# Masks of half of the first layer's score groups added by TensorE, normalised tokens also made by GpSimd, and a new order

## The chip, the cores and the metric

The kernel runs on one core of one Trainium2 chip. The metric is device time in microseconds (us) of one execution; lower is better. A core has five engines with an instruction queue each: TensorE (PE, matrix products into PSUM), VectorE (DVE), ScalarE (ACT), GpSimd (POOL) and SyncE (SP), which here issues all transfers (DMAs). Each engine works through its own queue in order and waits on semaphores where it needs another one's result. In the profile, PEld are PE's weight loads.

## The reference

Two layers, each a sliding-window attention and a token-mixing MLP, on one sequence of 2048 tokens of width 512:

```python
def _A_ref(x, wqkv, wo):
    B, S, D = x.shape
    H = 32; Dh = D // H; W = 256
    qkv = (x @ wqkv).reshape(B, S, 3, H, Dh).transpose(2, 0, 3, 1, 4)
    q, k, v = qkv[0], qkv[1], qkv[2]
    scores = jnp.einsum("bhqd,bhkd->bhqk", q, k) * (Dh ** -0.5)
    idx = jnp.arange(S)
    mask = (idx[:, None] - idx[None, :] >= 0) & (idx[:, None] - idx[None, :] < W)
    p = _softmax(jnp.where(mask[None, None], scores, -1e9), axis=-1)
    o = jnp.einsum("bhqk,bhkd->bhqd", p, v)
    return o.transpose(0, 2, 1, 3).reshape(B, S, D) @ wo

def _B_ref(x, w1, b1, w2, b2):
    h = _layernorm(x, axis=-1)
    u = _gelu(jnp.einsum("bsd,sf->bdf", h, w1) + b1)
    y = jnp.einsum("bdf,fs->bds", u, w2) + b2
    return y.transpose(0, 2, 1)

x = A_x
x = x + _A_ref(_layernorm(x, axis=-1), A_wqkv, A_wo)
x = x + _B_ref(_layernorm(x, axis=-1), B_w1, B_b1, B_w2, B_b2)
x = x + _A_ref(_layernorm(x, axis=-1), A_wqkv, A_wo)
x = x + _B_ref(_layernorm(x, axis=-1), B_w1, B_b1, B_w2, B_b2)
```

Data are bfloat16. The MLP mixes tokens: its first product runs over the 2048 tokens (w1 is 2048 x 1792), its second one gives 2048 tokens back.

## The kernel before

The kernel is written as a graph. Every piece of work is an `op` with an engine, a function that issues its instructions, what it reads and what it writes. The lists `alts` name other engines that could do the same work. A constant, `ORDER`, holds one order of all ops, and for each op which of its alternatives is taken; `replay` reads it, gives out buffers from pools (8 PSUM banks, 7 buffers `pt` of probabilities, and so on) in that order, and `emit` writes each engine's instructions in that order with the semaphore waits that the dependencies and reused buffers ask for. So the order of the work on every engine is written out by hand, as it were, in `ORDER`; nothing is reordered at run time. The `cost` values serve whoever makes the order and have no effect on the chip.

**Attention of a layer.** The queries are cut into chunks: in layer 0 two of 4 blocks of 64 queries and three of 8 (`CHUNKS`, numbered 0 to 4), in layer 1 four of 8. Heads are worked on in four sets `o` of 8 heads. For a chunk, `attention_plan` lists groups of key block by query block tiles: each group fills two pairs of PSUM banks. One score group is one op `f_sc` (matmuls at L679): for each piece four matmuls that run side by side in four row tiles of 32 rows (two heads of 16 each, the keys spread block-diagonally in `kbd`), into four banks. Then come two exponentials on ACT (L694), each over two banks, which write `pt`; then the masks (`f_mask`, L715) on GpSimd, which multiply the diagonal and the far-edge blocks by 0 or 1; then the product with the values (`f_pv`, L732) on PE. A layer has 76 score groups. The pair of each plan's entry `(c0, n, w0)` says where a mask lies and which of its forms it takes. After the products: a transpose on DVE (L752), reciprocal, scaling (`prod`, L758, on GpSimd or DVE), a second transpose, and the output projection (`wo_block`), whose result is added to `x_sb` (L774).

**Around it.** `ln_blocks` computes token statistics (L464, L466, DVE), the inverse deviation (`rstd`, L477, GpSimd) and the normalised tokens `xh_sb` (`normalise`, L484, DVE). `qkv` transposes them (by transfer, or by PE at the start of a layer), projects to q, k and v with matmuls at L506, copies the results out of PSUM (`evq`, `evk`, `evv`, on DVE or ACT) and spreads the keys: for the first 512 tokens of a layer straight from PSUM (`evka`, L574 on ACT, L575 on DVE), later from a staging buffer `stg` into `kbd` (`kz`): by eight small transfers (L595), or by two multiplications with the constants `par` (L600) on GpSimd or DVE. In layer 0 the transfers are allowed for the last quarter of the tokens only.

**Filling PE.** Between score groups PE gets other matmuls, all through the helper at L506: projections, output projections, the first MLP product over the tokens that are ready (`u_part`, evicted at L838 or L842), and in layer 1 the second product of the MLP of layer 0 (`y_block`). After a layer's attention come the rest of the first product (`u_last`, L853, with an addition at L864 and the gelu at L868) and the second product, whose weights are loaded into `pt` and `w2b`; `w2b` holds the partial sums of the first product before that.

Of the kernel before, what the change touches and what calls it, by code (L numbers as in the profile page):

```python
# [7 lines left out]
dt = mybir.dt  # L8
# [3 lines left out]
P = 128  # L12
# [3 lines left out]
    'c-qZYJ&5Dl6~40X%xYimfEE<c1_ks$3o7(L4;)aTLJJCLK>;l&phATU2NZCjfD0ukpa&{ks1U)03KvsM;lhOjQ@C*9VgfE)xNzaZg$ox`xNyLQ3l}-^-'  # L16
    ';DQ%9mqm*W-MJ@-Jf&5^PTUig=m&x8#EXp8bY!nO0MoWh9R2vM_t$7>+eNTltlTbIJQ3qL12EE&*!#1FRrHR{$V`+Fha<*Oj8l@rpfWY<@rHtgZr|~gK'
    '>GZ*|u*d({`H+-*Ru$I5mFHahx4wJ(M<^t+x1172kzX9J-<IS(;`TvM8#W`cBnkFhyRoV8VDjhMOcwGf6@i{tULAvv-6L*7t>4BNl`W%dRJnj#HaVxcO'
    'qaSa6l)qabixrBc~$CzHu^!aeM8wOVCpLhES0nCW_#*=7vWZfDv2$Jsnhr|ERcfK@6w%wQOa836zT_zipG$yi!RnIcu~kI94m_aQR`pSV89{oIJ^e&GA'
    '9y6=af|HhRACumQ@C=84oTo2hWtT&rXYlr9FZ03VS^*BkAKShxjhGDfDR9Ti`s<mp>gS}kabzF|KRvO3Y`V7r>`qrzC$2!Lhw>uapn~Y}Yx>!KPFu$}~'  # L20
    'ih@)%QS0^k!Z!gXr2ucGz_|I`^Nf4L=yna$ghYuVw|!Ho@RdAgnT+Q}G0RvsV{^iCc}_Dev}<i!0PLpL?am3gdov!>H1i0y-E9lkG0yYcvMl#;y<YEj?'
    'i-q3JO9#kSl*0Q>rHfjAN9KT_q|@XJABh0K6E;rp5r+A?H$hD{1yzTrE^>>*Evmt6_YTDqO6r=lC;ZO{AMGh6(Cy>hCw4-HX7hf&=`#*iHP-Tt(Gae7b'
    '{v|GO8d5^73(6Q5Fk%AG1uzVAxkxRqA#n3AW-mo<OLn>$<f#iQ@zsp6e>LS}hC}1t65GqTp3Ml_jbw+cx5)$E^;WtEif$DfF1_GfYoW6uQ$9@7jhba$1'
    '_Ex(y58G+L<9P#`114?H0}u#JaFg2?f_B1tkkkffW8-5ZTDAxR>N49kdUyWNrv#C5}RP=c^J+<^id*OwP^zYk9woA*+TX}aBR!$1c1Oec%QqNrAS{F=V'
    'MzrXDbI0*6XmIlf~uUzksN5Zs6=)^Qa8j=e<)+?-1p;ek5jXG5*bQ&?~U?5-`vl+%I%9F%mQ5Yf&WUAvjt7?veWL48;SrA3X^=L&FAiV+-bPe&UAh{Sa'
    '<@<5J-_K)#t=u&|K@?OpKmj2_jRZl(^ZnE_UBW6vCa3`kVIWt6WS9mZC@+^Z;yCjIXn_DKk>?#r$}*16vg|GNX(Jrp@q8e^<>;*C;*{rQ`KKfaQKME13'
    'O=}m7@%32r2(mR=vWsF?RL8Wf5EU@AY8iv<^@63Qz}sQD1z`Uj4co*Q^l&tfmaAog2!_RAxvb9u_7x=(81Y!Ay22v<phRIr_(*=v?K$eP`j<^T9(POVH'
    'iB&I3|Lc5C7Ij>-E3euzQyM!}tG8M3_*mDHX*LWN{fqI{jC}SglqIK~U|PstT<BzDI+mth(K-^BP)t9=FEyfa)aR2ObOtAPDvV=t>5Cqcc$|but>YwFi'
    'd51S5uLwBCK;RxfHs5fo4qwOUO!1-Do>=?#*E9S)l*G>xoF)tb#Z10`02@};ri`o7h0dCx0Zjli^v(glPhPBbyERcnk5Wb^>s-&ufaWoZg{7R=`s6b;m'
    '^U-wmARQmnxbgHWVRDrz;EU+~;n@qRtUkr#=({&IdMK`QCj&*(GC%%u6rfs)z{IK4vHy{tH`m^#ESe8vSI4|C_%21K|EfDx_(z9(FMlehSDeZJ+pob(5'  # L30
    '2Dea(495WP3W%^y>-u&FoLQ|ph2465({)=spTYFFnM%I_wF9drwK#_StX0;FBFC|JmSHt43&FYd-as~R#dR#mqVHG^a$On~XIjOyfLA^btcNpEqiJjnh'
    'r<oW0f$XPmZ3n@G>$Q78OESuD3TR8Yiv@TP60lQ#u^$q#*W+&b=6Z5Jtt6oV6Pu0!-R}LA^U?qg~9>qclsURDh(($@9rA6KqI=<3TWCp$knxD+kiTRoI'
    '94KJFcKZ)OtnJK%{`8Bn*EPLImUu0}}9p0M3G}xP`3|64$XhSJnAyJ_F{d>SQvT&wwY!aA?eCvwJ8`rgN*1cAgUiP^T&QpCV+WgwZq=v|g?L(IMFL;bg'
    'LG3(#HJhN2iIl4VW?gcleKzrGcC1~JS{H%UR*NCUnMs3Z(0+l>#nAXG(gK{UcG0~LzK@N~Z~Os5EAlq{2oF$&x@%l15!c6;}}?}0MpQ55^w4}u12AlIo'
    'v+8oma4x0!Bnide|p`llJ1@WoId0t)Q6gb~xUaIf{ASx+hu7Q^|fyavNSQ5?C^v1@RiFm>;@k*8(8?@nl9syS4>9n>0V(Tk7N<h+q?_-QdkHhU^Ydk#c'
# [270 lines left out]
def bass_interleave_layers__sliding_block__mixer_token_mlp__prompt_kernel(  # L306
# [12 lines left out]
    F = B_w1.shape[1]  # L319
    assert S == 2048 and D == 512 and F % 256 == 0  # L320
    NT = S // P
    NC = 4
    NFT = F // P
    EPS = 1e-5
    SMSCALE = 0.25
    NPT = 7
    NRL = 4
    NVS = 4
    SPLIT = [True, False]

    CHUNKS = [[(0, 4), (4, 4), (8, 8), (16, 8), (24, 8)], [(0, 8), (8, 8), (16, 8), (24, 8)]]
# [642 lines left out]
```

## Time and profile before

| what | us |
| --- | --- |
| median of 3 runs | 441.83 (441.41 to 443.33) |
| the profiled execution | 441.94 |
| its span on the core | 440.2 |
| first score group starts | 8.77 |
| last score group of layer 0 / layer 1 starts | 151.34 / 352.7 |
| ACT, exponentials: 304, mean of one | 281.5 busy, 1.042 |
| PE, stretch 150 to 200, between the layers | 50.00 busy of 50 |

The span is the time between the first and the last instruction on the core. Layer 0's attention takes roughly the first 155 us, the rest of its MLP about 45, layer 1's attention, with the second product of layer 0's MLP among it, up to 355, and its own MLP the rest. Groups of instructions are named by line, engine, operation and output<-input tile.

The page's slices (each 11 us; a digit is the busy share in tenths) show the stages:

```profile
PE   7998998999999999999999999999999999999996
...
DVE  6999888887887678475768868899987746512223
ACT  5999999999999913618999999999999950420000
POOL 2687898778677610011574877877666631000000
```

### The profile page before, as it was taken

To read this page: it belongs to the slowest core of one execution; us is meant where nothing else is said; L and a number is where in the kernel's file an instruction comes from. 1 tells how busy PE (TensorE), PEld (TensorE's weight loads), DVE (VectorE), ACT (ScalarE), POOL (GpSimd) and SP (SyncE) were. 2 spreads that over 40 slices of the span, in tenths; PEclk is the share of its full clock that TensorE was granted. 3 is DMA by queue.
4 is the path that set the end of the run, shared out by engine and by line. 5 is a ranking of instruction groups with operands and counts; after the bars stand their busy time and mean duration, and the time that the engine had idled before them with its cause. 6 is when DMAs were issued, how large, how long until landed. Compare 5 with 4: busy or idle time off the path is not lost.

```text
span 440.2 us, 13923 instructions
## 1 busy us (share of the span) xinstructions
PE 422.9 (96%) x5992; PEld 187.6 (43%) x5992; DVE 311.1 (71%) x570; ACT 318.5 (72%) x364; POOL 225.4 (51%) x344
## 2 busy tenths in 40 slices
PE   7998998999999999999999999999999999999996
PEld 6543333344333444444444444443443444434452
DVE  6999888887887678475768868899987746512223
ACT  5999999999999913618999999999999950420000
POOL 2687898778677610011574877877666631000000
PEclk9999999999999999999999999999999999999999
DMA  7752423203225365533351651140223346773513
GB/s 243 206 96 64 112 51 66 60 13 72 44 43 147 106 177 158 145 99 78 92 112 37 140 118 25 47 102 17 51 60 86 90 132 179 205 200 112 157 53 101
DMA packets 99885, 45.09 MB, mean 102 GB/s; under 512 B 30064, under 2 KB 99824, under 8 KB 99824
## 3 DMA queue, kind: packets, MB, share of 16 engines
q1 hardware_dynamic: 99824, 44.21, 39.2%
q8 instruction: 47, 0.77, 0.7%
q14 instruction: 14, 0.11, 0.1%
HBM read 33.56 MB, written 2.10 MB: 81 GB/s over the span
## 4 chain that ended last, share of the span: by engine, by line
PE 71%; ACT 19%; DVE 3%; POOL 3%; DMA 2%; issue 1%; SPq 0%; DVEq 0%
PE PS L506 49%; ACT pt L694 19%; PE PS L853 8%; PE PS L679 7%; PE PS L732 7%; POOL pt L715 3%; DMA w2b<-in_B_w_dram 2%; DVE stats L464 1%; DVE rl L752 1%; DMA x_sb<-in_A_x_dram 0%; DVE xh_sb L484 0%; DVE x_sb L774 0%; PE PS L542 0%; DVE vst L620 0%; DVE x_sb L894 0%
## 5 line engine op out<-in xcount | busy, mean ns | idle before, releaser
L694 ACT ACTIVATE pt<-PS 128x1024 bf16<-128x1024 f32 (+1 forms) x304 | 281.5, 1042 | 11.8 <-PE PS L679 9.6
L715 POOL TENSOR_TENSOR pt<-pt,ldm 128x256 int32<-128x256 int32 (+1 forms) x270 | 177.2, 682 | 78.9 <-ACT pt L694 78.4
L506 PE MATMUL PS<-uT,w2b 128*128 128x512 bf16 (+1 forms) x294 | 69.7, 370 | 1.1 <-DMA w2b<-in_B_w_dram 0.9
L506 PE MATMUL PS<-xhT,wqkv 128*128 128x512 bf16 (+1 forms) x288 | 67.1, 358 | 2.7 <-ACT pt L694 0.8
L506 PE MATMUL PS<-xh_sb,w1b 128*128 128x512 bf16 x280 | 69.0, 381 | 0.4 <-ACT pt L694 0.3
L679 PE MATMUL PS<-qT,kbd 32*128 32x256 bf16 (+4 forms) x1488 | 60.7, 252 | 5.5 <-ACT pt L694 3.7
L477 POOL TENSOR_TENSOR rstd<-agg,mhalf 128x2 f32<-128x2 f32 (+1 forms) x33 | 23.2, 703 | 58.8 <-DVE agg L466 55.9
L894 DVE SCALAR_TENSOR_TENSOR x_sb<-PS,b2col,x_sb 128x512 bf16<-128x512 f32 x31 | 22.9, 744 | 40.8 <-PE PS L506 40.6
L679 PEld LDWEIGHTS PS<-qT,kbd 32*128 32x128 bf16 x1488 | 21.7, 93 | 65.1 <-ACT pt L694 44.8
L752 DVE STREAM_TRANSPOSE rl<-PS 128x1024 f32<-128x1024 f32 x32 | 39.7, 1240 | 13.3 <-PE PS L732 12.8
L868 ACT ACTIVATE uT<-rl,b1col 128x512 bf16<-128x512 f32 x28 | 18.7, 714 | 39.9 <-DVE rl L864 39.9
L732 PE MATMUL PS<-pt,vb 64*17 64x320 bf16 (+4 forms) x2976 | 43.0, 252 | 2.1 <-DVE x_sb L774 0.6
L464 DVE BATCH_NORM_STATS2 stats<-x_sb 128x6 f32<-128x512 bf16 x64 | 43.0, 680 | 2.2 <-DMA x_sb<-in_A_x_dram 1.5
L506 PEld LDWEIGHTS PS<-uT,w2b 128*128 128x128 bf16 x294 | 26.7, 98 | 33.6 <-issue 3.1
L506 PE MATMUL PS<-uT,pt 128*128 128x512 bf16 x168 | 40.9, 380 | 0.0
L732 PEld LDWEIGHTS PS<-pt,vb 64*17 64x17 bf16 x2976 | 31.3, 85 | 17.2 <-POOL pt L715 5.6
L506 PEld LDWEIGHTS PS<-xh_sb,w1b 128*128 128x128 bf16 x280 | 23.9, 98 | 32.1 <-issue 5.7
L853 PE MATMUL PS<-xh_sb,w1b 128*128 128x512 bf16 x168 | 37.0, 380 | 0.0
L506 PEld LDWEIGHTS PS<-xhT,wqkv 128*128 128x128 bf16 x288 | 23.9, 97 | 30.2 <-issue 6.0
L484 DVE TENSOR_SCALAR xh_sb<-x_sb,agg,rstd 128x512 bf16<-128x512 bf16 x64 | 30.6, 498 | 7.6 <-POOL rstd L477 7.6
L506 PE MATMUL PS<-wqkv,xhT 128*128 128x512 bf16 x128 | 34.4, 381 | 0.2 <-ACT pt L694 0.2
L506 PE MATMUL PS<-wo_sb,oT 128*128 128x512 bf16 x128 | 32.5, 381 | 0.3 <-DVE oT L763 0.2
(58 smaller groups left out, 313.1 us busy)
## 6 DMA issues: line engine op xcount, KB each, us to landing
w1b<-in_B_w_dram SPq DMA_DIRECT2D x112, 128.0 KB, 2.7
w2b<-in_B_w_dram SPq DMA_DIRECT2D x70, 128.0 KB, 2.6
pt<-in_B_w_dram SPq DMA_DIRECT2D x42, 128.0 KB, 3.0
vb<-vst SPq DMA_DIRECT2D x64, 68.0 KB, 2.1
out_dram<-x_sb SPq DMA_DIRECT2D x15, 128.0 KB, 1.8
x_sb<-in_A_x_dram SPq DMA_DIRECT2D x3, 512.0 KB, 8.1
wqkv<-in_A_wqkv_dram SPq DMA_DIRECT2D x4, 256.0 KB, 4.2
kbd<-stg SPq DMA_DIRECT2D x56, 16.0 KB, 2.0
```

The source lines that it names most:

```text
L464: op("vector:stat", lambda e: e.bn_stats(st[:, 0:6], x_sb[:, t, :]), reads=[f"x{t}"], writes=[("st", i)], cost=dve_cost(512))
L477: op("gpsimd:rstd", lambda e: e.tensor_tensor(rstd[:, t0:t1, 0], agg[:, t0:t1, 1], mhalf[:, 0:1].to_broadcast([P, t1 - t0]), op=ALU.pow), ...
L484: op("vector:xh", lambda e: e.tensor_scalar(xh_sb[:, t, :], x_sb[:, t, :], agg[:, t, 0:1], rstd[:, t, :], op0=ALU.subtract, op1=ALU.mult), ...
L506: return e.matmul(o, lhsT=w, rhs=x, start=start, stop=stop, skip_group_check=True)
L679: last = e.matmul(bank(tt[r // 2], r % 2)[:, base + c0 * 64:base + (c0 + n) * 64], lhsT=kbd[32 * r:32 * r + 32, tk.slot, o, jj].rearrange( ...
L694: op("scalar:exp", lambda e, ts=ts, tp=tp, i=i, cols=cols: e.activation(probs(tp)[:, i, 0:cols, :], pair(ts)[:, :, 0:cols].rearrange("p r ...
L715: return e.tensor_tensor(v, v, m, op=ALU.mult)
L732: last = e.matmul(bank(t, h)[32 * r:32 * r + 17, i + q0 * 64:i + (q0 + n) * 64], lhsT=vb[64 * h:64 * h + 64, tk.slot, jj, 4 * o + r, :], r ...
L752: op("vector:od", lambda e, t=tod, tr=tr: e.transpose(rl[:, tr.slot:tr.slot + 2].rearrange("p a b -> p (a b)"), pair(t)), reads=[(tod, i) ...
L853: last = e.matmul(bank(tu, tt), lhsT=v()[:, sc - b0, k0 + tt * P:k0 + (tt + 1) * P], rhs=xh_sb[:, sc, :], start=(sc == b0), stop=(sc == NT ...
L868: op("scalar:gelu", lambda e, ft=ft, tt=tt: e.activation(uT[:, ft, :], rl[:, tmps[tt].slot], ACTF.Gelu_apprx_tanh, bias=b1col[:, ft:ft + 1 ...
L894: op("vector:resy", lambda e: e.scalar_tensor_tensor(x_sb[:, t, :], bank(ft), b2col[:, t:t + 1], x_sb[:, t, :], op0=ALU.add, op1=ALU.add), ...
```

## The change

Four things change, and with them the constant `ORDER`, so the order of all ops is new, as is the choice among alternatives.

1. In layer 0, for the score groups listed in `BIASED` (chunk 1: the first two entries of the plan where they stand alone; chunks 2 and 3: entries 1, 2 and 4; chunk 4: entry 2), the masks are no longer multiplied in by GpSimd. PE adds a large negative number to masked scores in PSUM, ahead of the exponential: matmuls of a 0/1 selector `sel` with a table `bb` that holds 0 or -4e9, in the same four row tiles, accumulated on the scores. They are part of the op `f_sc`. Only the first piece of such a group sets the start flag.
2. `sel` and `bb` are built at the start, from a triangle `tri` that is now 192 wide: one fill on GpSimd, 12 small operations on DVE.
3. `normalise` may also run on GpSimd.
4. In layer 0, keys of the second and third quarter of the tokens may also be spread by transfers. Those fill only the diagonal blocks, so two of the three buffers of `kbd` are filled with zeros first, on GpSimd. The list of alternatives for layer 0 is GpSimd or DVE first.

```diff
+    MASKED = 4e9
...
+    BIASED = [{1: (0, 1, 2), 2: (1, 2, 4), 3: (1, 2, 4), 4: (2,)}, {}]
...
-        tri = sb("tri", [P, P])
+        tri = sb("tri", [P, 192])
+        sel = sb("sel", [P, 2, P])
+        bb = sb("bb", [P, 2, 2, 64])
...
+        op("gpsimd:zero", lambda e: e.memset(sel[:].rearrange("p a b -> p (a b)").bitcast(dt.float32), 0.0), writes=["sel"], cost=200)
+        BIAS_KEYS = []
+        for r in range(4):
+            g0, g1 = 32 * r, 32 * r + 32
+
+            def f_sel(e, g0=g0, g1=g1):
+                d, v = sel[g0:g1, 0, 0:32], ident[g0:g1, g0:g1]
+                (p, c), (q, _) = [[list(a) for a in x.ap] for x in (d, v)]
+                return e.tensor_copy(bass.AP(d.tensor, d.offset, [p, [160, 2], [64, 2], c]),
+                                     bass.AP(v.tensor, v.offset, [q, [0, 2], [0, 2], c]))
+            op("vector:sel", f_sel, reads=["ident", "sel"], writes=[("sel", r)], cost=150)
+            for i, (add, mul) in enumerate(((-1.0, MASKED), (0.0, -MASKED))):
+                def f_bb(e, g0=g0, g1=g1, i=i, add=add, mul=mul):
+                    v = tri[g0:g1, g0:g0 + 64]
+                    p, c = [list(a) for a in v.ap]
+                    return e.tensor_scalar(bb[g0:g1, :, i, :], bass.AP(v.tensor, v.offset, [p, [32, 2], c]), add, mul,
+                                           op0=ALU.add, op1=ALU.mult)
+                op("vector:sel", f_bb, reads=["tri"], writes=[("bb", r, i)], cost=150)
+                BIAS_KEYS.append(("bb", r, i))
+            BIAS_KEYS.append(("sel", r))
...
+        for k in (1, 2):
+            op("gpsimd:zero", lambda e, k=k: e.memset(kbd[:, k].rearrange("p a b c d -> p (a b c d)").bitcast(dt.float32), 0.0),
+               writes=["kz0"], cost=1900)
...
                op0=ALU.subtract, op1=ALU.mult),
-               reads=[f"x{t}", f"ag{t}", f"rs{t}"], writes=[f"xh{t}"], cost=dve_cost(512, 0.25, ptrs=2), lock=True)
+               reads=[f"x{t}", f"ag{t}", f"rs{t}"], writes=[f"xh{t}"], cost=dve_cost(512, 0.25, ptrs=2), lock=True,
+               alts=[("gpsimd", lambda e: e.tensor_scalar(xh_sb[:, t, :], x_sb[:, t, :], agg[:, t, 0:1], rstd[:, t, :],
+                                                          op0=ALU.subtract, op1=ALU.mult), 800)])
...
-                if not layer and m < 3:
-                    ways = ways[:0:-1]
-                op(ways[0][0] + ":kz", ways[0][1], reads=[ts] + [("par", h) for h in range(2)],
+                if not layer:
+                    ways = ways[:0:-1] + ways[:1]
+                op(ways[0][0] + ":kz", ways[0][1], reads=[ts, "kz0"] + [("par", h) for h in range(2)],
...
+                    on_pe = su[0][0] in biased and len(su) == 1
...
-                                        start=True, stop=True, tile_position=(32 * r, 0), skip_group_check=True)
+                                        start=fresh or not on_pe, stop=True, tile_position=(32 * r, 0), skip_group_check=True)
+                                fresh = False
+                        for c0, nc_, w0 in plan[su[0][0]][1] if on_pe else ():
+                            both = nc_ == 2 and w0 == 1
+                            for i in range(1 if both else nc_):
+                                far = w0 + i < 2
+                                for a in range(2):
+                                    lo = 32 if far and a else 0
+                                    hi = 128 if both and a else 96 if both else 32 if not far and not a else 64
+                                    for r in range(4):
+                                        last = e.matmul(
+                                            bank(tt[r // 2], r % 2)[:, (c0 + i) * 64 + lo:(c0 + i) * 64 + hi],
+                                            lhsT=sel[32 * r:32 * r + 32, a, :],
+                                            rhs=bb[32 * r:32 * r + 32, 1 - a].rearrange("p i n -> p (i n)")[
+                                                :, (0 if far else 64) + lo:(0 if far else 64) + hi],
+                                            start=False, stop=True, tile_position=(32 * r, 0), skip_group_check=True)
                         return last
...
-                    masks, mk = list(plan[su[0][0]][1]), []
+                    masks, mk = [] if on_pe else list(plan[su[0][0]][1]), []
```

By the order of instructions of both programs, engine by engine, the counts that differ are these (the rest of the work is the same, at other places of the queues):

| work | before | after |
| --- | --- | --- |
| PE: mask matmuls (32 / 64 / 96 columns) | 0 | 208 / 208 / 288 |
| GpSimd: masks | 270 | 202 |
| normalised tokens, DVE / GpSimd | 64 / 0 | 28 / 36 |
| spread of keys from `stg`, transfers / GpSimd / DVE (two instructions each on an engine, eight transfers) | 7 / 9 / 8 | 5 / 10 / 9 |
| first keys of a layer, ACT / DVE | 4 / 8 | 1 / 11 |
| scaling of the attention's output, GpSimd / DVE | 12 / 20 | 14 / 18 |
| copies of the first MLP product, ACT / DVE | 3 / 25 | 6 / 22 |
| key copies `evk`, ACT / DVE | 4 / 20 | 3 / 21 |

## The prediction

> **What bounds the kernel now.** I read the page first, then a table of busy time by stage, then the timeline around single score groups, the waits, and the order of instructions of both programs.
>
> ```profile
> span 440.2 us, 13923 instructions
> PE 422.9 (96%) x5992; PEld 187.6 (43%) x5992; DVE 311.1 (71%) x570; ACT 318.5 (72%) x364; POOL 225.4 (51%) x344
> ...
> L715 POOL TENSOR_TENSOR pt<-pt,ldm 128x256 int32<-128x256 int32 (+1 forms) x270 | 177.2, 682 | 78.9 <-ACT pt L694 78.4
> ```
>
> PE looks full everywhere, but its busy time hides waits (ends of matmuls are modelled), so I look by stage. Columns of the next view: stretch, its length, then busy us of PE, PEld, DVE, ACT, POOL, the granted clock, the DMA share and GB/s.
>
> ```profile
> 10.00:60.00 50.00, 45.05 (x912) 21.11 (x912) 46.98 (x98) 48.45 (x58) 37.93 (x57) 1.00 0.49 118
> 60.00:90.00 30.00, 27.26 (x606) 11.57 (x609) 24.50 (x43) 29.95 (x33) 24.15 (x37) 1.00 0.27 56
> 90.00:150.00 60.00, 58.37 (x1049) 24.11 (x1050) 48.29 (x83) 57.92 (x63) 44.91 (x67) 1.00 0.34 78
> 150.00:200.00 50.00, 50.00 (x349) 22.86 (x350) 34.88 (x67) 18.37 (x25) 7.44 (x11) 1.00 0.48 137
> 200.00:300.00 100.00, 99.99 (x1610) 42.07 (x1611) 75.31 (x130) 93.92 (x107) 65.96 (x99) 1.00 0.35 78
> ```
>
> Layer 0's attention (10 to 150) is ACT's: 30 of 30 us in the second stretch. In the first one DVE is nearly as full (46.98 of 50). Layer 1's (200 to 300) and all that follows an attention is PE's.
>
> The ACT limit at one score group, columns start, length, what:
>
> ```profile
> 56.17 1.96 ACT L694 ACTIVATE pt<-PS 128x1024 bf16<-128x1024 f32 x2
> ...
> 56.65 0.40 PE L679 MATMUL PS<-qT,kbd 32*128 32x64 bf16 x12
> ...
> 63.84 0.12 PEld L679 LDWEIGHTS PS<-qT,kbd 32*128 32x128 bf16 x8 [0.53 <-ACT pt L694]
> 63.85 0.40 PE L679 MATMUL PS<-qT,kbd 32*128 32x320 bf16 x8
> ```
>
> The second pair of rows: scores wait in PE's queue for an exponential to free PSUM banks, and what stands behind them waits too.
>
> **A yardstick.** Layer 0 has 76 score groups of two exponentials. I count rounds of five groups by the starts of their first score matmul. Two limits appear. ACT: the rounds that begin at 58.38 and 67.51 took 9.13 and 9.17 us with 0.05 and 0.00 us of idle ACT, so ten exponentials need 9.13. PE: the steady rounds of layer 1 (246.47, 256.46) took 9.99 with 30 full-size (512-column) matmuls beside scores and products, and one such matmul is 0.215 us (in the chain, eight take 1.83 and six 1.40). A round with n of them needs 9.99 - 0.215 (30 - n): 9.56 for 28, 8.27 for 22. From 18.95 to 143.07 layer 0's thirteen rounds took 9.38, 9.41, 9.70, 10.95, 9.13, 9.17, 9.17, 9.51, 10.00, 9.57, 9.38, 9.40, 9.36: 124.1 us. With their n (18, 22, 22, 28, 20, 18, 22, 26, 30, 28, 22, 22, 26) the larger limit, plus one ACT copy of 0.62 in the fourth and 0.37 in the first, explains all but 3.2 us: about 0.3 + 0.6 + 1.2 between 28 and 58, where DVE is full, 0.4 in the eighth and 0.7 in the last three.
>
> **The change, part by part.**
>
> *Masks on PE.* 36 of layer 0's score groups lose their GpSimd masks: the counts in the two programs are 270 and 202, so 68 go (56 of 128x256 at 745 ns, 12 of 128x128 at 460): 47 us of POOL. Nothing waits long for them (PEld on POOL pt: 5.6 us in all), so this alone gives little. In their place come 704 matmuls, 176 sets of four row tiles: 72 sets of 96 columns, 52 of 64, 52 of 32, 11,904 columns in all. The trace has the nearest thing, a score group of six short sets (the first row below): its sets of 64 columns start 28 to 29 ns apart when they follow each other, its 128 ones 57, that is columns / 2.4 GHz plus 2 ns, with their weight loads hidden. So 4.96 + 0.35 = 5.3 us of PE. The lower bound is 4.96; the upper is a weight load (93 ns, mean of the PEld row on qT,kbd) exposed at every set: 16.4 us. I take 5.3, because those score sets too change weights each time. The Trainium skill (TensorE: Matmul & The Clock Gate, "Wait — 56ns, not 53.3ns?") says that matmul starts never come closer than about 25 ns; taken for each of the 704 that would be an estimate of 17.6 us. The trace disagrees for row tiles (the four of a set start 3 to 4 ns apart); taken per set it adds about 0.5 us.
>
> ```profile
> 32.53 0.41 PE L679 MATMUL PS<-qT,kbd 32*128 32x64 bf16 x24
> ...
> L679 PEld LDWEIGHTS PS<-qT,kbd x1488: 89/93/95, 8.8 to 352.7; 32*128 32x128 bf16 x186
> ```
>
> A round of chunks 2 and 3 gets 1056 columns in 21 sets: 0.48 us; of chunk 4, 0.17; of chunk 1, 0.44. On the ACT-bound rounds this hides in the wait at the score's head. The loop there is exponential (1.04), 0.06 to the score, 0.46 from score to next exponential (56.65 to 57.10; 30.49 to 30.94), plus the added 0.13 to 0.19: 1.69 to 1.75, under ACT's 1.83 per group. On PE-bound rounds it is paid whole.
>
> *Normalised tokens on GpSimd.* 36 of 64 leave DVE; in layer 0's attention DVE keeps 6 of 26, and GpSimd makes the rest (18, and two ahead of the first score). One costs DVE 407 ns median and up to 1118, GpSimd about 0.69 to 0.72 (its nearest row, the key spread L600, 692 median). They lie behind masks in GpSimd's queue, and the transposing transfers behind them. Keys are ready early enough to cover that: the group at 76.68 uses keys spread by 62.32; without that cover each would cost its 0.7.
>
> The DVE row's tail is what a busy GpSimd costs: normalisations take 0.31 to 0.41 when none of its instructions overlaps, and mostly 0.7 to 0.9 where they overlap throughout.
>
> ```profile
> L484 DVE TENSOR_SCALAR xh_sb<-x_sb,agg,rstd x64: 314/407/1118, 4.7 to 369.8; 128x512 bf16<-128x512 bf16 x64
> ...
> L600 POOL TENSOR_SCALAR kbd<-stg,par x18: 682/692/1208, 40.9 to 282.6; 128x512 bf16<-128x512 bf16 x18
> ```
>
> The Trainium skill (SBUF — State Buffer, "Who interferes with whom") has an exclusive port lock for this pair; the row agrees, and it speaks for the change, as layer 0's GpSimd work falls from 132 masks to 64.
>
> In groups 0 to 35, DVE loses 14 normalisations (14 x 0.498 = 7.0 us) and gains four small set-up operations (0.2 each), one more key eviction (two of 0.47) and one more key spread (two of 0.35): net -4.5 of its 47 us. So the 2.1 us of stalls between 28 and 58 should mostly go.
>
> *New order.* After the change the rounds' n is 20, 22, 24, 22, 22, 20, 20, 26, 28, 28, 24, 22, 26. With the added sets the larger limit, and the same two ACT copies, gives 9.38 (as measured), 9.13, 9.18, 9.75, 9.13, 9.13, 9.13, 9.61, 10.04, 10.04, 9.13, 9.13, 9.30: 122.1, and 0.17 more for the last four groups (24 matmuls in both). So -1.9 us if all stalls go, +1.3 if all 3.2 stay. I take -1.7, by the relief of DVE.
>
> *Keys by transfers.* The order uses it less, not more: 40 issues instead of 56, two spreads in layer 0 where there were three. Two fills of the key buffer on GpSimd are added (about 1.8 us each, at the two memset rows' 0.2 for 128 elements and 0.1 for one); one stands ahead of the first rstd. Nothing is taken for the transfers.
>
> *Start.* Ahead of the first token statistics DVE now has six mask tables, one selector and a fill. Small DVE operations start 0.12 to 0.14 apart, 1.0 us; they need the triangle (GpSimd, done at 2.10 before), and 0.59 of idle waiting for x covers part. One projection (0.44) moves behind the first score group. I take +0.3, bounds 0 and +1.0.
>
> *Layer 1.* The work is the same; three double evictions leave ACT for DVE where PE is full: worth nothing. Its uneven last rounds (9.12, 9.28, 9.88, 9.26, 10.32 from 296.56) need 24, 24, 28, 26, 30: 0.9 us over the limits. With 24, 24, 26, 28, 30 I take -0.5, bounds -0.9 and +0.2.
>
> *Tail.*
>
> ```profile
> 380.00:400.00 20.00, 18.91 (x87) 8.01 (x86) 4.68 (x8) 5.45 (x9) 0.00 (x0) 1.00 0.67 190
> ...
> 388.81 1.47 PE L506 MATMUL PS<-uT,w2b 128*128 128x512 bf16 x6 [0.52 <-DMA w2b<-in_B_w_dram]
> ```
>
> PE waits 1.1 us there for weights that overwrite buffers just read. The new order puts some output matmuls ahead of the last of the first product, which covers these loads: -0.6, bounds -1.1 and +0.5.
>
> **Sum.** The profiled execution took 441.94 us (span 440.2; the median of the runs is 441.83, so nothing is corrected). +0.3 - 1.7 - 0.5 - 0.6 = -2.5: 439.4 us. All best -3.9, 438.0; all worst +3.0, 444.9.
>
> **Rivals.** *The stalls stay.* The waits between 28 and 58 come from the order of fillers and PSUM banks, not from DVE. For: ACT idles only 0.38 and 1.04 us in the third and fourth round, so what is to be won is small. Against: DVE's 94%. Then +1.3 + 0.3, with half of the other gains: about 443.0.
>
> *The added matmuls decide (slower).* Place: between score and exponential. If a set costs 93 ns, six sets are 0.56 and four 0.37; the loop becomes 1.56 + 0.56 = 2.12 and 1.93, 0.29 over 1.83 for 20 groups and 0.10 for 12, 7.0 us in all: 448. At 60 ns it is 0.09 x 20 plus 0.8 for each of three PE-bound rounds, 4.2: 443.6. It decides from 45 ns a set in the loop (1.83 - 1.56 = 0.27 for six). For: a set of 32 columns has only 13 ns in which to load the next weights, and no row shows such a set. Against: 28 ns at 64 columns.
>
> *GpSimd late (slower).* Tokens 2 and 3 are normalised there at the start, about 1 us later than now, and their transpose on PE moves earlier. If every early block lags by two such operations (1.4 us) at two places, with the start's bound: about 445.
>
> **Chances.** Forecast 0.48, of which 0.42 ends below 439.6; stalls stay 0.22; matmuls decide 0.23; GpSimd late 0.07. What a measurement of this kernel can tell is 0.5%, 2.2 us: faster 0.42, same 0.28, slower 0.30. The forecast's own range is 438.0 to 441. The range for all is 437.6 to 446.5: below the best bounds by a little, and up to between the two prices of the matmuls.
>
> **What would show it.** Starts of the added sets 15 to 42 ns apart; the rounds of layer 0 near 9.13, those with n of 28 near 10.04; DVE under 44 us in 10 to 60; the first score near 9; PE over 19.5 us in the twenty after the last first-product matmuls. I am wrong if ACT idles after scores in groups with added sets, or if rounds between 28 and 58 keep their length.

## The result, and the profile after

The changed kernel takes 483.49 us (median of 4 runs, 481.86 to 484.84), the kernel before 442.07 beside it: a ratio of 1.093, 95% interval 1.089 to 1.097. The forecast was 439.4 with a range up to 446.5. The profiled execution took 483.29 us with a span of 481.5.

Of the changed kernel's page, here are its head and two groups (line, engine, operation, output<-input, count; busy us and mean ns of one; idle us before it):

```profile
span 481.5 us, 15189 instructions
PE 427.5 (89%) x6623; PEld 197.0 (41%) x6696; DVE 307.9 (64%) x551; ACT 317.3 (66%) x360; POOL 260.3 (54%) x318
...
L763 POOL TENSOR_TENSOR pt<-pt,ldm 128x256 int32<-128x256 int32 (+2 forms) x202 | 131.1, 674 | 81.7 <-ACT pt L742 81.6
L515 POOL TENSOR_SCALAR xh_sb<-x_sb,agg,rstd 128x512 bf16<-128x512 bf16 x36 | 75.1, 2089 | 1.6
```

The masks fell from 270 to 202 on GpSimd, as forecast. But one normalisation on GpSimd takes 2.09 us, where 0.69 to 0.72 was forecast: 75 us, more than the 46 us of masks that it was rid of (177.2 - 131.1). The normalisation now stands in the chain of work that ended last, with 9% of the span; GpSimd as a whole has 17%. The chain by engine, before and after:

```profile
PE 71%; ACT 19%; DVE 3%; POOL 3%; DMA 2%; issue 1%; SPq 0%; DVEq 0%
```

```profile
PE 61%; POOL 17%; DVE 9%; ACT 6%; issue 3%; DMA 2%; POOLq 0%; SPq 0%
```

The same stretches as before the change (start and end, length, busy us of PE, PEld, DVE, ACT and POOL, the granted clock, DMA share, GB/s):

```profile
10.00:60.00 50.00, 40.87 (x926) 22.43 (x935) 38.08 (x83) 41.16 (x50) 40.07 (x38) 0.93 0.44 107
60.00:90.00 30.00, 25.34 (x683) 12.71 (x688) 22.27 (x43) 28.26 (x33) 20.60 (x21) 1.00 0.26 37
90.00:150.00 60.00, 49.91 (x1262) 23.75 (x1271) 42.42 (x70) 52.66 (x58) 33.27 (x39) 1.00 0.24 56
150.00:200.00 50.00, 45.92 (x608) 20.11 (x617) 31.67 (x56) 25.87 (x28) 21.51 (x28) 0.97 0.43 117
200.00:300.00 100.00, 96.32 (x1236) 41.69 (x1250) 68.61 (x121) 73.66 (x87) 56.27 (x74) 1.00 0.39 96
```

In the first stretch, of which the first 3.4 us now go by before the first score group, ACT falls from 48.45 to 41.16 busy, PE's matmuls from 45.05 to 40.87 and DVE from 46.98 to 38.08; GpSimd rises, from 37.93 to 40.07. No engine is full there: they wait for each other. The granted clock is 0.93 there; it was 1.00.

How a late GpSimd becomes a lost round is seen in the timeline of layer 1 (start, length, engine, line, operation; several instructions in a row are one line, the bracket is idle time before it):

```profile
334.59 4.13 POOL L515 TENSOR_SCALAR xh_sb<-x_sb,agg,rstd 128x512 bf16<-128x512 bf16 x2
...
338.68 4.99 POOL L763 TENSOR_TENSOR pt<-pt,ldm 128x256 int32<-128x256 int32 x8
338.78 5.04 DVE L512 TENSOR_SCALAR xh_sb<-x_sb,agg,rstd 128x512 bf16<-128x512 bf16 x1
...
342.71 1.67 PE L780 MATMUL PS<-pt,vb 64*17 64x64 bf16 x96 [2.08 <-ACT pt L742]
...
345.87 0.24 PEld L712 LDWEIGHTS PS<-qT,kbd 32*128 32x128 bf16 x12 [1.78 <-DVE vst L651]
```

Two normalisations hold GpSimd for 4.13 us. Eight masks pile up behind them and then run without a gap. For as long as they run, a DVE normalisation (0.407 us median) does not end: 5.04 us. The value eviction behind it on DVE is late, and PE waits for it before the next scores. The five score groups from 338.07 on took 15.5 us; the same five took 9.3 in the kernel before.

The start lost 4.6 us on its own:

```profile
2.01 2.14 DVE L472 TENSOR_SCALAR bb<-tri 32x128 bf16<-32x128 bf16 x1 [0.96 <-POOL tri L444]
...
2.31 1.80 POOL L482 MEMSET kbd<- 128x2048 f32 x1
...
6.36 0.68 DVE L492 BATCH_NORM_STATS2 stats<-x_sb 128x6 f32<-128x512 bf16 x1
```

The first table operation on DVE took 2.14 us, where the five behind it took 0.18 to 0.19 each: it ended when GpSimd's fill of the key buffer did. With the other tables the first token statistics begin at 6.36 instead of 2.95, and the first score group at 13.38 instead of 8.77.

### The profile page after: what moved, and what is told of

It is laid out like the page before. It is cut to its first block, busy times and chain, and to the rows that moved or that the text cites. A ratio compares the mean times of both kernels' runs of the same rounds, so it can differ in the third digit from the quotient of the medians.

```text
span 481.5 us, 15189 instructions
## 1 busy us (share of the span) xinstructions
PE 427.5 (89%) x6623; PEld 197.0 (41%) x6696; DVE 307.9 (64%) x551; ACT 317.3 (66%) x360; POOL 260.3 (54%) x318
## 4 chain that ended last, share of the span: by engine, by line
PE 61%; POOL 17%; DVE 9%; ACT 6%; issue 3%; DMA 2%; POOLq 0%; SPq 0%
PE PS L536 42%; POOL xh_sb L515 9%; PE PS L712 7%; ACT pt L742 6%; PE PS L780 6%; PE PS L901 6%; POOL pt L763 5%; DVE stats L492 2%; DMA xhT<-xh_sb 2%; DVE rl L800 1%; POOL rstd L505 1%; DVE xh_sb L512 1%; DVE x_sb L822 1%; PE PS L726 1%; DMA w2b<-in_B_w_dram 1%
## 5 line engine op out<-in xcount | busy, mean ns | idle before, releaser
L742 ACT ACTIVATE pt<-PS 128x1024 bf16<-128x1024 f32 (+1 forms) x304 | 282.7, 1033 | 43.6 <-PE PS L712 29.5
L763 POOL TENSOR_TENSOR pt<-pt,ldm 128x256 int32<-128x256 int32 (+2 forms) x202 | 131.1, 674 | 81.7 <-ACT pt L742 81.6
L515 POOL TENSOR_SCALAR xh_sb<-x_sb,agg,rstd 128x512 bf16<-128x512 bf16 x36 | 75.1, 2089 | 1.6
L536 PE MATMUL PS<-xh_sb,w1b 128*128 128x512 bf16 x259 | 66.9, 386 | 7.2 <-issue 6.1
L536 PE MATMUL PS<-uT,w2b 128*128 128x512 bf16 (+1 forms) x287 | 68.2, 369 | 0.8 <-issue 0.3
L780 PE MATMUL PS<-pt,vb 64*17 64x320 bf16 (+4 forms) x2976 | 44.3, 253 | 13.7 <-POOL pt L763 10.6
L901 PE MATMUL PS<-xh_sb,w1b 128*128 128x512 bf16 x164 | 37.7, 379 | 5.5 <-POOL xh_sb L515 5.2
L780 PEld LDWEIGHTS PS<-pt,vb 64*17 64x17 bf16 x2976 | 30.1, 85 | 29.3 <-POOL pt L763 11.9
L536 PEld LDWEIGHTS PS<-xhT,wqkv 128*128 128x128 bf16 x288 | 24.9, 102 | 32.5 <-issue 7.6
L536 PE MATMUL PS<-wqkv,xhT 128*128 128x512 bf16 x115 | 31.0, 386 | 2.4 <-issue 1.0
L536 PE MATMUL PS<-wo_sb,oT 128*128 128x512 bf16 x122 | 30.8, 380 | 0.8 <-issue 0.8
```

Source lines behind the costliest of these rows:

```text
L515: alts=[("gpsimd", lambda e: e.tensor_scalar(xh_sb[:, t, :], x_sb[:, t, :], agg[:, t, 0:1], rstd[:, t, :], op0=ALU.subtract, op1=ALU.mult) ...
L536: return e.matmul(o, lhsT=w, rhs=x, start=start, stop=stop, skip_group_check=True)
L742: op("scalar:exp", lambda e, ts=ts, tp=tp, i=i, cols=cols: e.activation(probs(tp)[:, i, 0:cols, :], pair(ts)[:, :, 0:cols].rearrange("p r ...
L763: return e.tensor_tensor(v, v, m, op=ALU.mult)
L780: last = e.matmul(bank(t, h)[32 * r:32 * r + 17, i + q0 * 64:i + (q0 + n) * 64], lhsT=vb[64 * h:64 * h + 64, tk.slot, jj, 4 * o + r, :], r ...
L901: last = e.matmul(bank(tu, tt), lhsT=v()[:, sc - b0, k0 + tt * P:k0 + (tt + 1) * P], rhs=xh_sb[:, sc, :], start=(sc == b0), stop=(sc == NT ...
```

## The experiments

All ratios are against the kernel before, run beside each on the same chip. "After" is the changed kernel.

**All normalisations on DVE, in the new order** (after; the order's choice for the 36 operations set to DVE).

```diff
-   36 of 64 xh: alternative 1 (gpsimd)
+   64 of 64 xh: alternative 0 (vector)
```

> The changed kernel with one edit: all 64 normalisations on VectorE, at the same places of the same order. Theory (a GpSimd normalisation takes 2.07 us where 0.7 was reckoned, and what queues behind it is late): 483 falls to 440 to 447; the late start (first score group at 13.4 instead of 8.8) stays, so not under 440. Rival A (the added mask matmuls and the new order cost most of it): it stays above 465. Rival B (the start and its effects on the clock are the main loss): it stays within 5 us of 483.

477.46 us, ratio 1.077 (1.073 to 1.080). Taking GpSimd's slow operation away recovers only 6 us, so the theory as written fell. The timeline shows one reason: the new order counts on GpSimd to have tokens ready. A block of 128 tokens is now normalised by DVE at 100.32, behind the copies in its queue, and PE waits 5 us for the transfer that transposes it:

```profile
100.32 0.53 DVE L511 TENSOR_SCALAR xh_sb<-x_sb,agg,rstd 128x512 bf16<-128x512 bf16 x1
...
104.68 2.74 PE L535 MATMUL PS<-xhT,wqkv 128*128 128x512 bf16 x6 [5.02 <-DMA xhT<-xh_sb]
```

So this run removes one fault and makes another; it did not isolate GpSimd's price.

**Only the masks on TensorE, in the old order** (before, with the added matmuls and tables; normalisation, key spreads and order as before).

```diff
+   f_sc: the 704 matmuls on sel and bb; sel and bb built behind the first statistics
```

> The kernel before with only the masks of the 36 score groups moved to TensorE, in the old order; the twelve set-up operations stand in VectorE's queue behind the first two tokens' normalisation. Theory: 439 to 445, as 5.3 us of added matmuls hide under ScalarE in layer 0. Rival A: 455 or more.

452.47 us, ratio 1.022 (1.019 to 1.025): by the ratio these masks alone lose 9.6 us. Layer 0's attention takes 154.78 us instead of 142.57, layer 1's the same as before. The granted clock is 0.999. PE stops in the middle of runs of matmuls that wait for nobody:

```profile
105.76 0.97 PEld L773 LDWEIGHTS PS<-pt,vb 64*17 64x17 bf16 x83 [0.42 <-issue]
105.76 1.19 PE L773 MATMUL PS<-pt,vb 64*17 64x64 bf16 x82
108.58 0.46 PE L773 MATMUL PS<-pt,vb 64*17 64x320 bf16 x14 [1.64 <-issue]
108.59 0.13 PEld L773 LDWEIGHTS PS<-pt,vb 64*17 64x17 bf16 x13 [1.85 <-issue]
```

"issue" means that the profile shows nothing the engine waited for. There are six such pauses in the trace where PE is idle for over 0.4 us; from one start to the next they last 0.65 to 1.94, 7.0 us together. The kernel before has none. They come at TensorE instructions number 1213, 1723, 2742, 4526, 5036 and 6310 of the record: the distances are 2, 4, 7, 2 and 5 times 255, to within one. The DMA queue named "instruction" moves 16,384 bytes at a time, once for each such block; before and in this run the page has

```profile
q8 instruction: 47, 0.77, 0.7%
```

```profile
q8 instruction: 53, 0.87, 0.9%
```

transfers and MB. In each of the six cases PE goes on 1.3 to 1.8 us after one of these transfers has landed. The reading that fits is that PE had run out of instructions: 704 matmuls and 704 weight loads are 5.5 blocks more, in a stage that is already made of short matmuls. But added matmuls are not needed for such a pause. Four of the runs below without any of them have one in layer 0 as well: 0.77 us in the run with the cheap form in the old order, and 1.5 us each, near 64 us, in those with parts of the new order that have all normalisations on DVE, the small operation on DVE, or the new order from group 137. The last of these stands at number 2241, which is 193 + 8 x 256 (its trace lacks no matmul record); the first of the six above is 193 + 4 x 255.

**Only the normalisations on GpSimd, in the old order** (before, the same 36 tokens).

```diff
+   alts=[("gpsimd", lambda e: e.tensor_scalar(..., op0=ALU.subtract, op1=ALU.mult), 800)]
```

> The kernel before with only the same 36 normalisations moved to GpSimd, in the old order, all masks on GpSimd. Theory: 36 times 1.4 us more than reckoned on a queue that is 51% busy, so 465 to 500, at least as slow as the changed kernel. Rival A: under 450.

497.85 us, ratio 1.125 (1.123 to 1.127): 55.5 us lost by this part alone, more than by the whole change. With the change around it the subtraction costs less: going to the cheap form (below) brings 30 us there and 40 us in the old order. Whether the new order or the masks taken off GpSimd make that difference was not separated.

**Four forms of the normalisation on GpSimd** (after; by token number, one run, so only the durations are used; the second form leaves the mean out, the third the deviation, the fourth adds the mean).

```diff
+   FORMS = [sub mean, mul rstd | mul rstd, add 0.0 | sub mean, mul 1.0 | mul rstd, add mean]
```

> The changed kernel with four forms of the normalisation on GpSimd, by token block modulo 4: subtract a per-partition value then multiply by one (as it is); multiply by one per-partition value and add a constant 0 (leaves the mean out); subtract one per-partition value and multiply by a constant 1 (leaves the deviation out); multiply by one and add the other (both used the other way round). If two per-partition values cost it, the second and third take about 0.7 us and the fourth 2.07. If the subtraction costs it, the first and third take 2.07, the second and fourth 0.7. If it is none of these, all take 2.07. The time falls with the number of cheap ones, to 455 to 470 if two of four are.

The one tile's instructions (minimum, median, maximum ns; first and last start):

```profile
L515 POOL TENSOR_SCALAR xh_sb<-x_sb,rstd x10: 687/691/696, 27.9 to 397.0; 128x512 bf16<-128x512 bf16 x10
L517 POOL TENSOR_SCALAR xh_sb<-x_sb,agg x9: 1998/2002/2131, 13.0 to 325.0; 128x512 bf16<-128x512 bf16 x9
L513 POOL TENSOR_SCALAR xh_sb<-x_sb,agg,rstd x9: 2070/2076/2210, 29.7 to 395.0; 128x512 bf16<-128x512 bf16 x9
L519 POOL TENSOR_SCALAR xh_sb<-x_sb,rstd,agg x8: 762/765/1198, 15.0 to 379.7; 128x512 bf16<-128x512 bf16 x8
```

The second value per partition costs 0.07 us. Subtract-then-multiply costs 1.3 more than multiply-then-add: 2.00 us against 0.69 with one value, 2.08 against 0.77 with two. Both steps differ between the two forms, so that it is the subtraction and not the multiplication in second place is likely but not shown; "the subtraction" below stands for the pair. The row that I had taken for nearest, the key spread, is a multiplication and an addition.

**The cheap form for all 36** (after).

```diff
-   tensor_scalar(xh, x, mean, rstd, op0=subtract, op1=mult)
+   tensor_scalar(xh, x, rstd, mean, op0=mult, op1=add)
```

> The changed kernel with all 36 GpSimd normalisations as a multiplication by the deviation and an addition of the mean (two values per partition as before, but no subtraction; it adds the mean where the reference subtracts it before the multiplication). Theory: the new order was made for a GpSimd normalisation of about 0.8 us and got 2.07; with the form measured at 0.76 it loses less than half: 483.5 down to 450 to 460, GpSimd 47 us less busy, DVE's longest normalisation under 2.5 us. Rival: the order itself or the added matmuls cost the time, since with all normalisations on DVE it was still 477: then 468 or more.

453.31 us, ratio 1.021 (1.017 to 1.025). This form adds the mean where it should be subtracted; only its time is of use. The theory is met: 30 us come back, and with them the long DVE operations go (longest 0.81 us instead of 5.04):

```profile
L515 POOL TENSOR_SCALAR xh_sb<-x_sb,rstd,agg x36: 756/768/1196, 13.0 to 381.4; 128x512 bf16<-128x512 bf16 x36
...
L512 DVE TENSOR_SCALAR xh_sb<-x_sb,agg,rstd x28: 366/410/808, 8.0 to 383.3; 128x512 bf16<-128x512 bf16 x28
```

**The cheap form and an early start** (the run before; seven table operations moved behind the statistics of token 3).

```diff
-   DVE: 6 x bb, 1 x sel, ..., stat 1, agg 1, stat 0, agg 0, ..., agg 3
+   DVE: stat 1, agg 1, stat 0, agg 0, ..., agg 3, 6 x bb, 1 x sel
```

> The kernel of the run before (cheap form), and the seven table operations that stand ahead of the first statistics on DVE moved behind the statistics of token 3. Theory: the first table operation waited 1.8 us for GpSimd's fill of the key buffer, and with the six others it made the first score 4.6 us late; moved, the first score starts at 9.0 to 9.8 instead of 13.4, and the whole gains 3 to 4.5 us over the run before. Rival: the late start is caught up later, or the tables then come late for the first group that needs them: gain under 1 us.

451.93 us, ratio 1.017 (1.013 to 1.021). By the medians the gain is 1.4 us, and the two intervals overlap; by the profiled executions it is 4.3 (453.72 to 449.43). The trace has the mechanism: statistics at 2.84, and the first scores at 9.23, 4.14 us earlier.

```profile
2.84 0.69 DVE L491 BATCH_NORM_STATS2 stats<-x_sb 128x6 f32<-128x512 bf16 x1
...
9.23 0.40 PE L711 MATMUL PS<-qT,kbd 32*128 32x256 bf16 x12 [0.32 <-ACT qT L595]
```

**A quarter of the added matmuls** (the run with the masks alone; one row tile of four in each set).

```diff
-                                    for r in range(4):
+                                    for r in range(1):
```

> The kernel of before with the masks on TensorE in the old order, with only one of the four row tiles in each added set: 176 matmuls instead of 704, the same columns one after the other; three quarters of these groups' heads go unmasked. Theory: TensorE runs out of instructions, because a 16 KB block of 256 of them is used up in under about 3 us, which is what fetching the next takes; with 1056 instructions fewer the pauses of 0.65 to 1.9 us go, and 452.5 comes down to 444 to 447. Rival: the added columns ahead of the exponentials, or the lost or shifted masks on GpSimd, cost the time: 450 to 453, since the columns one after the other stay.

449.25 us, ratio 1.012 (1.008 to 1.016): 4.3 us of the 9.6 go. That lies between the two expectations. Of the pauses two are left, 0.70 and 1.60 us. Three quarters of these groups' heads stay unmasked in this run.

**The cheap form in the old order** (before; 36 normalisations on GpSimd as multiplication and addition).

```diff
+   alts=[("gpsimd", lambda e: e.tensor_scalar(..., op0=ALU.mult, op1=ALU.add), 800)]
```

> The kernel of before with the same 36 normalisations on GpSimd in the old order, in the cheap form (multiplication and addition; adds the mean). Theory of the form: of the 56 us lost with the subtraction 36 x 1.3 = 47 go at most, 450 to 465. Rival: in the old order the masks of all groups stand ahead of the normalisations in GpSimd's queue, and a cheaper form does not help: 475 or more. A third way, that it gains on before: under 441.

457.69 us, ratio 1.030 (1.025 to 1.035), against 1.125 with the subtraction: 41 of the 55 us go. The form is the main cost in both orders.

**All added matmuls, one column wide** (the run with the masks alone).

```diff
+                                    hi = lo + 1
```

> The kernel of before with the masks on TensorE in the old order, all 704 added matmuls kept but each only one column wide; the masks of these groups are mostly left out. Theory (instructions): the number of instructions is that of the full masks, so the pauses at the 16 KB blocks stay, 449 to 454, against 452.5 with full columns. Rival (columns): 11,904 columns go, 5.0 us of TensorE ahead of the exponentials; then about that much less, 445 to 448. With a quarter of the instructions and all columns it was 449.3.

450.68 us, ratio 1.017 (1.014 to 1.020). Taking away all but 704 of the columns brings 2.2 us, taking away three quarters of the instructions 4.3; the intervals of the two ratios overlap, so this order of the two is likely, not shown. Three pauses are left, 4.4 us together. Each run gains about what its pauses lost in the profiled execution (2.6 us here, 4.7 in the run before last). From the first score matmul to the start of the last added one, a group with six sets takes 0.41 us with everything, 0.40 with a quarter of the matmuls and 0.37 with one column; the scores alone take 0.19. A set has a price of its own, and the columns hardly matter.

**The exact normalisation in the cheap form** (early start; one small GpSimd operation makes minus mean times deviation ahead of each).

```diff
+   op("gpsimd:shift", tensor_scalar(shift, mean, rstd, -1.0, op0=mult, op1=mult))
+   ... tensor_scalar(xh, x, rstd, shift, op0=mult, op1=add)
```

> The changed kernel with the table operations behind the statistics of token 3 and the 36 GpSimd normalisations as a multiplication and an addition, exact this time: one more GpSimd operation of one value per partition makes minus mean times deviation ahead of each. Theory: 451.9 as with the inexact form, plus at most 36 x 0.1 to 0.2 us of GpSimd, nearly all hidden: 450 to 455. Rival: the wait between the small and the large operation delays keys: over 458.

453.31 us, ratio 1.023 (1.021 to 1.026). As expected: it costs 1.4 us more than the inexact form by the medians, 2.7 by the ratios.

**The early start and cheap form, without the added matmuls** (new order).

```diff
-                        for c0, nc_, w0 in plan[su[0][0]][1] if on_pe else ():
+                        for c0, nc_, w0 in ():
```

> The kernel with the cheap form and the early tables, in the new order, without the 704 added matmuls: the masks of these 36 score groups are left out altogether, GpSimd does not get them back, and the tables are still made. Theory: all that is left of the loss in layer 0 comes from the added matmuls (their time between score and exponential where filler matmuls stand ahead of the group, and the pauses for instructions): layer 0's attention falls from 151.7 to 142 to 144, the whole to 439 to 443, a ratio of 0.993 to 1.002. Rival: the new order's fillers cost it by themselves: layer 0's attention stays over 147, ratio over 1.006.

442.68 us, ratio 0.999 (0.997 to 1.000). In this run nobody masks these 36 groups. The theory is met, at the upper edge: layer 0's attention falls from 151.68 to 144.08. The same two score groups, with the added matmuls (the first view) and without:

```profile
43.62 0.40 PE L711 MATMUL PS<-qT,kbd 32*128 32x192 bf16 x8
...
43.85 0.30 PE L725 MATMUL PS<-bb,sel 32*128 32x96 bf16 x16
...
44.12 1.85 PE L779 MATMUL PS<-pt,vb 64*17 64x64 bf16 x128
...
44.22 1.94 ACT L741 ACTIVATE pt<-PS 128x1024 bf16<-128x1024 f32 x2 [0.16 <-PE PS L725]
...
45.40 0.27 PEld L779 LDWEIGHTS PS<-pt,vb 64*17 64x17 bf16 x25 [0.25 <-issue]
...
45.90 0.40 PE L711 MATMUL PS<-qT,kbd 32*128 32x128 bf16 x12
...
46.57 1.02 ACT L741 ACTIVATE pt<-PS 128x1024 bf16<-128x1024 f32 x1 [0.41 <-PE PS L725]
```

```profile
40.45 5.90 ACT L741 ACTIVATE pt<-PS 128x1024 bf16<-128x1024 f32 x6
...
42.92 0.40 PE L711 MATMUL PS<-qT,kbd 32*128 32x192 bf16 x8
...
43.41 1.53 PE L779 MATMUL PS<-pt,vb 64*17 64x64 bf16 x128
...
44.88 0.40 PE L711 MATMUL PS<-qT,kbd 32*128 32x128 bf16 x12
```

Without them the second score group follows after 1.96 us and ACT runs six exponentials without a gap. With them it follows after 2.28, and ACT, which needs 1.83 a group, idles 0.16 and 0.41. Two things are in this. The product between the two groups, the same 128 matmuls, takes 1.85 us instead of 1.53: TensorE stops in it for 0.33 us from one start to the next, at its instruction number 1723, where the run with the masks alone also stops, 1.2 us after a 16 KB transfer has landed. That is the whole 0.32 by which the second group comes later. The sets show between a group's first score matmul and its exponential: 0.60 us with four sets and 0.67 with six, where the prediction read 0.46 off the trace before. So the first gap is the sets' (0.14 of 0.16), and of the second about 0.3 is the pause and 0.1 the sets, an estimate from these starts.

The trace with the added matmuls has five such pauses in layer 0, at numbers 1213, 1723, 2743, 5037 and 6311: 0.84, 0.33, 1.67, 1.23 and 0.92 us, 5.0 together. The trace without them has none. So pauses can be up to 5.0 of the 7.6 us that layer 0 loses to the added matmuls, and sets ahead of late exponentials are the rest.

**Parts of the new order alone.** Five kernels take the order of before up to a point and the new one from there, with masks, keys and layer 0 as before.

```diff
-   order of before
+   order of before up to the point, then the order of after
```

From layer 1 on, with 13 exact cheap normalisations on GpSimd:

> The kernel of before up to the first score group of layer 1, and the new order (with 13 exact cheap normalisations on GpSimd) from there on. Theory: what is good in the change is its order of layer 1 and the tail: in the run with the cheap form and the early start these took 1.2 and 2.1 us less than before; so 438 to 440.5 beside a before of 442 to 443.5, a ratio of 0.990 to 0.996. Rival: the gain hung on what layer 0 left behind, ratio 0.998 or more.

443.39 us, ratio 1.001 (0.999 to 1.003): nothing gained, so the rival held. The same with all on DVE:

> As the run before, with all normalisations on DVE: only the order of layer 1 and the tail is new. Theory: the new order counts on GpSimd, and DVE on its own is late at one or two blocks of tokens, as in the run with all normalisations on DVE (layer 1's attention 158.1 against 151.5): 443 to 447. Rival: the order alone brings the gain: ratio under 0.996.

448.36 us, ratio 1.012 (1.010 to 1.014): the order needs GpSimd, as the theory said, and by more than it said. With the small operation on DVE, once for a block:

> The kernel of before up to layer 1, the new order from there with 13 exact cheap normalisations on GpSimd as in the earlier run, but minus mean times deviation is made on DVE once for a block of tokens (9 operations) instead of once a token on GpSimd (13 of 0.265 us). Theory: the small GpSimd operation ahead of each took the 1.3 us that layer 1's attention lost against the inexact form (152.8 against 151.5): ratio 0.994 to 0.998. Rival: the gain is not to be had, ratio 1.000 or more.

450.32 us, ratio 1.016 (1.013 to 1.018): a miss. GpSimd's normalisations waited 10.3 us in all for the small DVE operation, which stands in DVE's queue behind other work. From score group 112 on, and from 137 on:

> The kernel of before up to score group 112, the new order from there (9 exact cheap normalisations on GpSimd, the small operation on GpSimd). Theory: of the new order only the end gains: the part from the last score group on took 82.6 to 83.5 us with cheap normalisations against 84.7, and groups 132 to 147 29.1 against 29.5; the 1.3 us that moving six more matmuls between the layers cost is left out. So 0.7 to 2.2 us gained: ratio 0.995 to 0.998. Rival: 0.999 or more, the gain hangs on what came earlier.

445.59 us, ratio 1.006 (1.003 to 1.008): a miss.

> As the run before, with the new order from score group 137 on (4 exact cheap normalisations on GpSimd). Theory: the tail alone, 1.2 to 2.1 us: ratio 0.995 to 0.997. Rival: 0.999 or more.

441.90 us, ratio 0.9975 (0.9957 to 0.9992): the only exact kernel here with a gain on before that the interval shows, 0.25%. That is just outside what was expected (0.995 to 0.997). From the last score group on it takes 86.2 us instead of 87.5 in the profiled execution; layer 0, in its old order, holds the pause of 1.5 us named above there.

## Why the prediction was wrong

The stages by the trace, in us, from the starts of score groups and the span:

| stage | before | after | cheap form | and early start | and no added matmuls |
| --- | --- | --- | --- | --- | --- |
| to the first score group | 8.77 | 13.38 | 13.37 | 9.23 | 9.23 |
| layer 0's attention | 142.57 | 161.22 | 151.61 | 151.68 | 144.08 |
| to layer 1's first score group | 48.59 | 52.59 | 49.84 | 49.84 | 49.88 |
| layer 1's attention | 152.75 | 164.01 | 151.74 | 151.51 | 151.49 |
| the rest | 87.52 | 90.31 | 85.44 | 85.43 | 85.41 |
| span | 440.2 | 481.5 | 452.0 | 447.7 | 440.1 |

Taken away in this order, the 41.3 us divide into 29.5 for the subtraction on GpSimd, 4.3 for the start, 7.6 for the added matmuls, and -0.1 for all the rest. By the medians of the runs the three steps are 30.2, 1.4 and 9.2, by their ratios 32, 2 and 8. In another order the shares would differ: in the old order the subtraction alone costs 40.

- *Normalised tokens on GpSimd: the step that failed.* The prediction priced one at 0.69 to 0.72 by "its nearest row, the key spread". It took 2.09. The sum gave it no upper bound, as it did for the masks: the mask and the spread are GpSimd rows of like size, but neither does this arithmetic, and nothing in the trace before bounded it from above. The step also said that keys are ready early enough to cover a late one. That looked at one group (76.68) and not at the masks behind the normalisation in the same queue, on which PE's products wait (PE's matmuls stood 10.6 us idle for masks in the changed kernel). Its rival "GpSimd late" named the engine and got 0.07, with a price made of the same 0.7.
- *Relief of DVE.* Taken as -1.7 in layer 0. Part of it is there once the other faults are gone: without the added matmuls the four rounds from group 6 took 38.07 us by the trace, where before they took 39.44; that it is DVE's relief was not tested apart from the new order. But the first six groups, in which the new order does matmuls worth 30 full ones instead of 28, took 12.47 instead of 10.18, so layer 0 as a whole gained nothing. The port lock, quoted as speaking for the change, went against it: masks in a backlog leave no gap, and DVE waited through eight of them. (Layer 0's masks fall from 134 to 66 by the traces, not from 132 to 64.)
- *Start.* Taken as +0.3, bounds 0 to 1.0; it was +4.6. The sum counted eight DVE operations and noted that one fill stands ahead of the first rstd on GpSimd. It did not put the two beside each other: the first of the tables ended only with the fill of 1.8 us. The five others started 0.11 to 0.22 us apart, where 0.12 to 0.14 was reckoned.
- *Masks on TensorE.* The sets start 25 to 44 ns apart, half of them within 29, where 15 to 42 was forecast, and some rounds hide them: of those forecast at 9.13 with added sets, two took 9.30 and 9.17 with the cheap form and the early start. Two others took 10.35 and 11.14, of which 0.84 and 1.67 are pauses. Two things were missed. Instructions were counted as free: the pauses. And the yardstick took the larger limit over five groups, but the scores are only one group ahead of ACT; where PE comes late to a group, ACT waits for its sets whatever the round's mean says. The prediction's own sign of being wrong, ACT idle after scores in groups with added sets, came true. "The added matmuls decide" had the right place, not the right price; it ranged from 443.6 to 448, and the masks alone measure 452.5. (The 7.0 us it works out, put on the forecast of 439.4, make 446.4; where the rest of its 448 comes from is not said.)
- *Layer 1 and tail.* With the cheap form right in sign: -1.3 (-0.5 was taken) and -2.1 (-0.6). With the exact form in place of it layer 1's attention gains nothing (152.83) and the rest 1.3 (86.27). The new order gives back 1.3 between the layers, where it does six more matmuls, 1.5 in layer 0 and 0.5 at the start.

What stays open: why just these instruction blocks come late and others, used up as fast, do not; and how the 9.6 us of the masks divide exactly between pauses and late scores, since a pause can be absorbed by ACT's lead. Part of the large step may be the clock: the four runs of the changed kernel had granted clocks of 0.986, 0.975, 0.972 and 0.972 and spans of 480.1, 481.5, 481.9 and 483.1 us. Carried on to 1.0 in a straight line, that is an estimate of 5 us; no run separates it.

## What to carry to other kernels

Before moving an operation to another engine, find a row of the very same arithmetic on that engine; the same shape and type are not enough. Look at what stands behind it in that engine's queue, and whether a backlog there can shut out a neighbour. When a change adds many tiny matmuls, count sets and instructions as well as columns, and judge a stage group by group if the buffers between its engines hold only one group.

## What the hardware showed that was not expected

- A GpSimd operation on 128x512 bf16 with a per-partition value takes 0.69 us as multiply, then add, and 2.00 as subtract, then multiply.
- A DVE normalisation can stay shut out over several GpSimd instructions: 5.04 us beside eight masks in a row (4.99). The Trainium skill (SBUF — State Buffer, "Who interferes with whom") has the loser blocked until the other instruction ends; here it ended only when the whole row of them had.
- TensorE seems to run out of instructions at times: pauses of 0.65 to 1.94 us at multiples of 255 recorded instructions, each ended 1.3 to 1.8 us after a 16 KB transfer. The Trainium skill (Runtime: NRT & Kernel Launch, "Instruction fetch mechanics") has blocks of 256 instructions, and says that crossing one is mostly hidden; the distances agree with it to within one. The kernel before shows no such pause; with matmuls added in sets of four there are six, and four runs without them have one each.
- The granted clock fell to 0.75 between 340 and 350 us, where PE was busy for only 5.65 of 10, and to 0.80 between 10 and 20, after the late start (0.975 over the span); with the cheap form it is 0.992, and below 0.99 in the first 20 us only.
